# Linear attention followed by a mish feed-forward on one Trainium2 core: quarter-array key sums, later requests for v, reordered output products, a split first unit

## The chip, the cores and the metric

The kernel runs on one core of one Trainium2 chip. The metric is the device time in microseconds of one execution. A core has five engines with queues of their own: TensorE (PE, matmuls; its weight loads are listed as PEld), VectorE (DVE), ScalarE (ACT), GpSimd (POOL) and SyncE (SP, which here issues every DMA). Each engine works its queue in order and waits on semaphores for the others.

## The reference

q, k and v have 8 batches, 8 heads, 576 positions and 64 channels. Both q and k go through a feature map, and the attention is linear:

```
proj = x @ w_phi                                   # 64 -> 128 features
proj = proj - max(|proj|) over the features
phi  = concat(exp(proj), exp(-proj))               # 256 features
kv   = sum over s of phi(k)[s] * v[s];  z = sum over s of phi(k)[s]
out  = (phi(q) @ kv) / (phi(q) . z + 1e-6)
```

The result, as 4608 tokens of 512 channels, goes through a feed-forward: h = x @ w_in (512 to 2048), g = h * tanh(softplus(h)), out = g @ w_out (2048 to 512). Everything is float32.

## The kernel before

**Attention.** Two heads are handled together, so there are 32 head pairs of 576 keys. All keys of all pairs are laid end to end and cut into 144 tiles of 128 keys; a *unit* is four tiles (512 keys), and there are 36 units. A pair has 4.5 tiles, so every ninth tile holds 64 keys of one pair and 64 of the next: 16 such shared tiles. For unit n, `k_load` brings the keys (L270), `k_proj` multiplies them with w_phi into PSUM (L281, `project` L239, eight matmuls of 64 rows by 128 columns), `k_center` takes the maximum and subtracts it (L284, `center` L248, two VectorE operations over 1024 columns), `k_exp` makes both exponentials on ScalarE (L287), and `k_sum` adds phi(k) times v into the PSUM tile of the pair (L292). v has a column of ones behind its 64 channels, which gives z. Each matmul of `k_sum` is split by `halves` (L256) into two parts of 128 rows by 64 columns. A shared tile is run twice over its 128 rows, once for each pair; the host has put zeros into v where a key belongs to the other pair. `k_store` copies a finished pair to SBUF (L306). Queries go through the same steps (`q_load` to `q_store`), with transposes (`q_turn`, `q_out`) around the product with kv (`q_num`).

v is loaded a pair at a time by `v_load` (L274) into one of three buffers; keys and queries have three buffers each, the projection has two PSUM buffers (tag pp).

**Weights.** While attention runs, the feed-forward weights are converted into a high and a low part, 32 pieces in all (`weight_load` L135, `weight_ops` L140). Pieces with fp >= 2 are written to DRAM when both parts are there (`done` L223, store in L228) and come back later.

**Feed-forward.** A float32 product is made of three: high times high, high times low, low times high. `ff_in` (L435) makes h with seven block products, `first_product` and `winograd` combine them, `mish` applies the activation on ScalarE, `g_hi` (L509, ScalarE) and `g_lo` (L515, VectorE) split g into gh and gl, and `ff_out` (L561) multiplies with w_out. For each half (`which`) it fills two PSUM tiles with six products each, in the order gh wh, gh wl, gl wh, for the two blocks f of g.

**The order of the work** is written out by hand. Every step is an event with a nominal time, `at(time, step, ...)`; the events are sorted by it and issued in that order (L858 to L860), so the times set only the order on each engine's queue. The tables at L32 to L62 hold these times: L_AT for the four units ahead of the steady state (LEAD), K_AT and Q_AT for the key and query steps of a unit, which come STEP = 7.43 apart, CONV and WORD_AT for the weights, XS_AT and STEP1_AT for the feed-forward. The events of a unit are made in L685 to L715. All DMAs go through SP's one queue in this order, each with its own wait for a free buffer.

Of the kernel before, what the change touches and what calls it, by code (L numbers as in the profile page):

```python
# [12 lines left out]
ALU = mybir.AluOpType  # L13
# [24 lines left out]
Q_AT = (1.54, 3.27, 6.19, 6.49, 1.9, 3.04, 6.65, 10.0)  # L38
T_AT = (0.95, 2.0, 4.9, 5.3, 8.55, 10.92, 12.6, 13.1)
JOIN = 1.22  # L40
PRE = (11.72, 6.53)
CONV = (13.32, 14.93)
WORD_AT = 4.8
X0_AT = (37.79, 30.51)
RESUME = 38.35
FFSTEP = 10.6
HALF = 4
# [3 lines left out]
NXC = 9  # L51
FF2STEP = 8.01
TRAIL = 8.53
STEP1_AT = (0.75, 1.5, 1.53, 2.24, 5.7, 8.0, 6.24, 11.5, 12.7, 14.3, 18.4, 24.05)
XS_AT = (1.0, 10.69, 0.03, 4.92, 1.2)
# [13 lines left out]
def attention_then_mish(ctx, tc, qT, kT, va, w_phi, w_in, w_out, w_out2, out):  # L69
# [15 lines left out]
    nc.sync.dma_start(w_phi2, w_phi)  # L85
    ident = const.tile([P, P], F32, tag="ident", name="ident")
    make_identity(nc, ident)

# [51 lines left out]
    def weight_ops(kind, fp, k, quiet):  # L140
# [5 lines left out]
        def w():  # L146
            return piece[key][1][:, 0:4].rearrange("p b m -> p (b m)")
# [88 lines left out]
        return ops, rest_ops  # L236


    def project(raw, name):  # L239

        ps = ps_a.tile([P, 2, 4, F], F32, tag="pp", name=f"pp_{name}")
        for n in range(4):
            for j in range(2):
                rows = slice(j * D, (j + 1) * D)
                nc.tensor.matmul(ps[:, j, n], raw[rows, n * P:(n + 1) * P], w_phi2[rows], start=True, stop=True)  # L245
        return ps

    def center(ps, name):  # L248
        e = att.tile([P, 2, 2, 512], F32, tag="e", name=f"e_{name}", bufs=5)
        m = att.tile([P, 2, 4], F32, tag="m", name=f"m_{name}", bufs=4)  # L250
        nc.vector.tensor_reduce(m, ps, axis=AX.X, op=ALU.max, apply_absolute_value=True)  # L251
        nc.vector.tensor_tensor(e[:, :, 0, :].rearrange("p j (n f) -> p j n f", f=F), ps,  # L252
                                m.unsqueeze(3).broadcast_to([P, 2, 4, F]), op=ALU.subtract)
        return e

    def halves(ps, lhsT, rhs, start, stop):  # L256
# [8 lines left out]
    def pairs_of(t):  # L265

        for p in range(t * P // S, (t * P + P - 1) // S + 1):
            yield p, t - p * S // P

    def k_load(n):  # L270
        k_live[n] = att.tile([P, 512], F32, tag="kraw", name=f"kraw_{n}", bufs=3)
        nc.sync.dma_start(k_live[n], kT[n])

    def v_load(n):  # L274
        for t in range(4 * n, 4 * n + 4):
# [3 lines left out]
                    nc.sync.dma_start(v_live[p].rearrange("p t j w -> p (t j w)"), va[p])  # L279

    def k_proj(n):  # L281
        k_live[n] = project(k_live.pop(n), f"k_{n}")

    def k_center(n):  # L284
        k_live[n] = center(k_live.pop(n), f"k_{n}")

    def k_exp(n):  # L287
        e = k_live[n]
        nc.scalar.activation(e[:, :, 1, :], e[:, :, 0, :], AF.Exp)
        nc.scalar.activation(e[:, :, 0, :], e[:, :, 0, :], AF.Exp, scale=-1.0)  # L290

    def k_sum(n):  # L292
        es = k_live.pop(n)
        for i in range(4):
            for p, slot in pairs_of(4 * n + i):
                if slot == 0:
                    kv_ps[p] = ps_b.tile([P, 2, 2, VW], F32, tag="b", name=f"kvps_{p}")
                ps, vt = kv_ps[p], v_live[p]
                for j in range(2):
# [261 lines left out]
    def ff_out(n, which):  # L561
        s, sc, fp, first, last = steps[n]
        gh, gl = g_live[n]
        assert not any(("out", fp, k) in pieces_left for k in range(2))
        if first and which == 0:
            o_live[s] = [None] * 4
        assert stage[n, "u"] == 7
        for tt in (2 * which, 2 * which + 1):
            if first:
                o_live[s][tt] = ps_b.tile([P, DM], F32, tag="b", name=f"o_{s}_{tt}")  # L570
            ps = o_live[s][tt]
            cols = slice(tt % 2 * P, (tt % 2 + 1) * P)
            for f in range(2):
                wh, wl = wout[fp][:, f, 0], wout[fp][:, f, 1]
                h, l = gh[:, 2 * f + which, cols], gl[:, 2 * f + which, cols]
                for k, (g, w) in enumerate(((h, wh), (h, wl), (l, wh))):
                    nc.tensor.matmul(ps, g, w, start=(first and f == k == 0), stop=(last and f == 1 and k == 2))  # L577
        if which:
            del g_live[n]

# [167 lines left out]
    for i, pc in enumerate(pieces):  # L748
# [5 lines left out]
        at(clock - 12.0, weight_load, *pc)  # L754
        bits, sums = weight_ops(*pc, quiet)
        for delay, op in bits:
            at(clock - WORD_AT + delay, op)
# [141 lines left out]
```

## Time and profile before

| | us |
|---|---|
| median of 3 runs | 1041.77 (1040.81 to 1042.14) |
| profiled execution, its own time | 1043.07 |
| span of that execution, first to last instruction | 1041.3 |
| PE busy in the span | 1023.5 |
| DVE busy | 732.7 |
| ACT busy | 497.4 |
| POOL busy | 302.0 |

A line of the timeline gives the start in us, the duration, the engine, the line of the kernel, the operation, the tile written and the tiles read, the shape, and how often; in brackets stands the idle time of the engine ahead of it and what ended it. A line of the waits gives the engine and line that waited, what it waited for, the us in total, how many times, and the longest. "issue" is a wait for nothing that the profile shows. A line of the windows gives for a stretch from A to B its length and then the busy us of PE, PEld, DVE, ACT and POOL, each with a count, the granted TensorE clock (PEclk, 1.00 is full), the busy share of the DMA engines, and GB/s. A float32 matmul of the attention stage is two records in the trace, each with a weight load and a matmul.

### The profile page before, as it was taken

To read this page: it belongs to the slowest core of one execution; us is meant where nothing else is said; L and a number is where in the kernel's file an instruction comes from. 1 tells how busy PE (TensorE), PEld (TensorE's weight loads), DVE (VectorE), ACT (ScalarE), POOL (GpSimd) and SP (SyncE) were. 2 spreads that over 40 slices of the span, in tenths; PEclk is the share of its full clock that TensorE was granted. 3 is DMA by queue.
4 is the path that set the end of the run, shared out by engine and by line. 5 is a ranking of instruction groups with operands and counts; after the bars stand their busy time and mean duration, and the time that the engine had idled before them with its cause. 6 is when DMAs were issued, how large, how long until landed. Compare 5 with 4: busy or idle time off the path is not lost.

```text
span 1041.3 us, 27535 instructions
## 1 busy us (share of the span) xinstructions
PE 1023.5 (98%) x11848; PEld 970.8 (93%) x11848; DVE 732.7 (70%) x1158; ACT 497.4 (48%) x861; POOL 302.0 (29%) x263
## 2 busy tenths in 40 slices
PE   7999999999999999999999999999999999999998
PEld 7999899998989999999999999999999999999997
DVE  5888888887646987486674763367667677677665
ACT  4777777777754534344343533243333333333332
POOL 0545326533610555446553540000000000000000
PEclk9999999999999999999999999999999999999999
DMA  6545646666769576664855559982451542532621
GB/s 193 191 140 184 202 154 239 241 208 204 260 233 394 199 283 220 211 227 157 295 223 185 197 178 351 386 336 92 165 192 59 196 158 85 203 127 97 223 82 41
DMA packets 87081, 208.58 MB, mean 200 GB/s; under 512 B 6960, under 2 KB 34736, under 8 KB 84144
## 3 DMA queue, kind: packets, MB, share of 16 engines
q1 hardware_dynamic: 86960, 206.83, 56.4%
q8 instruction: 93, 1.52, 0.6%
q14 instruction: 28, 0.23, 0.1%
HBM read 122.91 MB, written 83.89 MB: 199 GB/s over the span
## 4 chain that ended last, share of the span: by engine, by line
PE 97%; DVE 1%; issue 1%; ACT 1%; DMA 0%; SPq 0%; DVEq 0%
PE h L449 34%; PE o L577 19%; PE o L598 17%; PE kvps L260 7%; PE num L260 7%; PE pp_k L245 4%; PE dt L328 3%; PE pp_q L245 3%; PE xt L371 2%; DMA kraw<-kT 0%; DVE m_k L251 0%; ACT L504 0%; DVE e_k L252 0%; DVE e_q L252 0%; DVE gl L518 0%
## 5 line engine op out<-in xcount | busy, mean ns | idle before, releaser
L449 PE MATMUL h<-xc,win 128*128 128x256 f32 x3024 | 381.5, 283 | 0.3 <-DVE u L477 0.3
L449 PEld LDWEIGHTS h<-xc,win 128*128 128x128 f32 x3024 | 375.3, 192 | 6.1 <-DVE u L477 0.5
L577 PE MATMUL o<-wout,gh 128*128 128x512 f32 x576 | 180.4, 395 | 0.2 <-ACT gh L512 0.2
L656 POOL TENSOR_TENSOR part<-part,du 128x512 f32<-128x512 f32 x18 | 23.4, 1298 | 387.9 <-DVE du L648 387.9
L577 PEld LDWEIGHTS o<-wout,gh 128*128 128x128 f32 x576 | 104.4, 190 | 18.7 <-ACT gh L512 0.4
L481 DVE TENSOR_TENSOR u<-h,u 128x512 f32<-128x512 f32 x72 | 49.6, 689 | 95.0 <-PE h L449 94.9
L577 PE MATMUL o<-wout,gl 128*128 128x512 f32 x288 | 112.8, 392 | 1.9 <-DVE gl L518 1.9
L598 PE MATMUL o<-wa,gh 128*128 128x256 f32 x576 | 104.4, 282 | 0.0
L456 ACT COPY p<-h 128x256 f32<-128x256 f32 x72 | 26.4, 367 | 134.0 <-PE h L449 134.0
L598 PEld LDWEIGHTS o<-wa,gh 128*128 128x128 f32 x576 | 88.6, 190 | 0.1
L260 PE MATMUL kvps<-v,e_k 128*64 128x65 f32 x2560 | 82.9, 224 | 4.0 <-issue 4.0
L260 PEld LDWEIGHTS kvps<-v,e_k 128*64 128x64 f32 x2560 | 79.3, 139 | 5.1 <-issue 4.4
L598 PE MATMUL o<-wa,gl 128*128 128x256 f32 x288 | 80.2, 283 | 0.0
L598 PE MATMUL o<-wb,held 128*128 128x256 f32 x648 | 79.3, 282 | 0.2 <-DVE du L648 0.2
L598 PEld LDWEIGHTS o<-wb,held 128*128 128x128 f32 x648 | 78.3, 188 | 0.4 <-DVE du L648 0.4
L334 ACT ACTIVATE e_q<-dt 128x512 f32<-128x512 f32 x144 | 74.3, 604 | 6.9 <-PE dt L328 6.8
L260 PE MATMUL num<-kv,e_q 128*64 128x65 f32 x2304 | 74.9, 223 | 0.0
L260 PEld LDWEIGHTS num<-kv,e_q 128*64 128x64 f32 x2304 | 70.1, 137 | 4.4 <-issue 0.3
L469 DVE TENSOR_TENSOR u<-h,p 128x256 f32<-128x256 f32 x72 | 30.2, 419 | 60.7 <-ACT p L456 60.7
L577 PEld LDWEIGHTS o<-wout,gl 128*128 128x128 f32 x288 | 54.4, 189 | 14.3 <-DVE gl L518 2.4
L251 DVE TENSOR_REDUCE m_k<-pp_k 128x8 f32<-128x1024 f32 x36 | 44.0, 1222 | 28.7 <-PE pp_k L245 28.7
L497 ACT ACTIVATE sb<-h 128x256 f32<-128x256 f32 x36 | 13.8, 384 | 105.0 <-PE h L449 71.1
(94 smaller groups left out, 1662.5 us busy)
## 6 DMA issues: line engine op xcount, KB each, us to landing
xc_spill<-xc SPq DMA_DIRECT2D x63, 512.0 KB, 4.6
xc<-xc_spill SPq DMA_DIRECT2D x63, 512.0 KB, 5.3
x<-x_spill SPq DMA_DIRECT2D x22, 512.0 KB, 7.0
o_part<-part SPq DMA_DIRECT2D x11, 1024.0 KB, 5.0
part<-o_part SPq DMA_DIRECT2D x11, 1024.0 KB, 5.9
in_spill<-wst_in SPq DMA_DIRECT2D x12, 896.0 KB, 4.4
win<-in_spill SPq DMA_DIRECT2D x12, 896.0 KB, 8.0
v<-va SPq DMA_DIRECT2D x32, 325.0 KB, 3.5
```

The costliest lines, as they stand in the source:

```text
L245: nc.tensor.matmul(ps[:, j, n], raw[rows, n * P:(n + 1) * P], w_phi2[rows], start=True, stop=True)
L251: nc.vector.tensor_reduce(m, ps, axis=AX.X, op=ALU.max, apply_absolute_value=True)
L260: nc.tensor.matmul(ps[rows], lhsT[:, rows], rhs[h], start=start, stop=stop, skip_group_check=True)
L328: nc.tensor.transpose(ps[:, i * P:(i + 1) * P], e[:, 0, i * P:(i + 1) * P], ident)
L334: nc.scalar.activation(e[:, s, :], ps, AF.Exp, scale=2.0 * s - 1.0)
L449: nc.tensor.matmul(ps, w, x, start=(i in (0, 2) and m == 0), stop=(m == 5), skip_group_check=True)
L456: nc.scalar.copy(p1, h_live[n][0][:, 0])
L469: nc.vector.tensor_tensor(u2, hx[:, 1], u_live[n][0], op=ALU.add)
L481: nc.vector.tensor_tensor(u[:, 0:3:2] if second(n) else u[:, 1:3], hy, u2.unsqueeze(1).broadcast_to([P, 2, CH]), op=ALU.add)
L577: nc.tensor.matmul(ps, g, w, start=(first and f == k == 0), stop=(last and f == 1 and k == 2))
L598: nc.tensor.matmul(ps, g, w, start=(start and k == 0), stop=(stop and k == 2), skip_group_check=True)
L656: nc.gpsimd.tensor_tensor(cross, cross, d_live[s, tau][0].unsqueeze(1).broadcast_to([P, 2, CH]), op=ALU.add)
```

## The change

Four edits, with retimed events.

1. `k_sum` takes the tiles of a unit with one pair first and the shared tile last. In a shared tile rows 0 to 63 go to the first pair and rows 64 to 127 to the second, as matmuls of 64 rows by 64 columns, in turn.
2. LOAD_AT sets the times of the loads: k_load at 11.1 ahead of the unit's time (before: 1.5 x 7.43 = 11.1), v_load at 1.0 ahead (before: 0.8 x 7.43 = 5.94), q_load at 9.59 (before: 8.92), the weights' words at 12.68 (before: 12.0). The store of a converted weight piece is two DMAs: the high part when it is written, the low part when that is.
3. `ff_out` makes all eight products with gh, and then the four with gl.
4. The first two tiles' columns of the first key unit come with w_phi in one DMA (`head`), the other two by k_load(0). The first unit is projected into two PSUM buffers, and centered and exponentiated in two halves.

The tables L_AT, K_AT, Q_AT, T_AT, CONV, X0_AT, XS_AT, STEP1_AT, LEAD_STEP and JOIN get other values. On PE's queue this moves one step: the projections of unit 4 and of the first query come ahead of k_sum(2). On ACT's queue mish(n, 1) comes ahead of first_product(n + 1) in most feed-forward steps, and on VectorE's some x_sum, x_block and drain steps change places with their neighbours.

```diff
-LEAD_STEP = 3.28
-L_AT = (0.0, 0.95, 3.4, 7.0, 9.38)
+LEAD_STEP = 2.8
+L_AT = (0.0, 2.62, 3.19, 7.71, 9.38)
-K_AT = (0.94, 1.9, 3.04, 3.85, 4.24)
+LOAD_AT = (-11.1, -1.0, -9.59, -12.68)
+K_AT = (0.94, 1.9, 3.62, 3.69, 4.24)
-JOIN = 1.22
+JOIN = 0.99
-X0_AT = (37.79, 30.51)
+X0_AT = (38.06, 28.03)
...
-    w_phi2 = const.tile([P, F], F32, tag="w_phi", name="w_phi2")
-    nc.sync.dma_start(w_phi2, w_phi)
+    head = const.tile([P, 3, F], F32, tag="head", name="head")
+    nc.sync.dma_start(head, w_phi)
+    w_phi2 = head[:, 0]
...
             nc.scalar.copy(dst[:, 0], piece[key][1][:, 1:8] if blocks else w())
+            spill(0)
...
+            spill(1, dst)
+
+        def spill(h, dst=None):
+            dst = piece[key][3] if dst is None else dst
             if fp >= 2:
...
-                nc.sync.dma_start(where, dst.bitcast(F32))
+                nc.sync.dma_start(where[:, h], dst[:, h].bitcast(F32))
...
+        for a, b, ps in parts:
+            nc.vector.tensor_reduce(m[:, :, a:b], ps[:, :, a:b], axis=AX.X, op=ALU.max, apply_absolute_value=True)
+            nc.vector.tensor_tensor(to[:, :, a:b], ps[:, :, a:b],
+                                    m[:, :, a:b].unsqueeze(3).broadcast_to([P, 2, b - a, F]), op=ALU.subtract)
...
+    def cuts_of(n):
+        return (0, 4) if n else (0, 2, 4)
...
     def k_sum(n):
         es = k_live.pop(n)
-        for i in range(4):
-            for p, slot in pairs_of(4 * n + i):
-                if slot == 0:
+        tiles = [list(pairs_of(t)) for t in range(4 * n, 4 * n + 4)]
+        for i in sorted(range(4), key=lambda i: len(tiles[i])):
+            fresh = []
+            for p, slot in tiles[i]:
+                if p not in kv_ps:
                     kv_ps[p] = ps_b.tile([P, 2, 2, VW], F32, tag="b", name=f"kvps_{p}")
-                ps, vt = kv_ps[p], v_live[p]
-                for j in range(2):
-                    for s in range(2):
-                        halves(ps[:, j, s], es[:, j, s, i * P:(i + 1) * P], (vt[:, slot, j, :],) * 2,
-                               start=(slot == j == s == 0), stop=(slot == 4))
+                    fresh.append(p)
+            shared = len(tiles[i]) == 2
+            for j in range(2):
+                for s in range(2):
+                    for r, (p, slot) in enumerate(tiles[i]):
+                        rows = slice(r * D, (r + 1) * D) if shared else slice(0, P)
+                        halves(kv_ps[p][:, j, s], es[rows, j, s, i * P:(i + 1) * P], (v_live[p][rows, slot, j, :],) * 2,
+                               start=(p in fresh and j == s == 0), stop=(slot == 4))
...
+        for g, ks in ((gh, (0, 1)), (gl, (0,))):
+            for tt in (2 * which, 2 * which + 1):
+                cols = slice(tt % 2 * P, (tt % 2 + 1) * P)
+                for f in range(2):
+                    for k in ks:
+                        nc.tensor.matmul(o_live[s][tt], g[:, 2 * f + which, cols], wout[fp][:, f, k],
...
-        at(t - 1.5 * STEP, k_load, u)
-        at(t - 0.8 * STEP, v_load, u)
+        at(t + (LOAD_AT[0] if u >= LEAD else -11.1), k_load, u)
+        at(t + (LOAD_AT[1] if u >= LEAD else -5.9), v_load, u)
...
-        at(t - 1.2 * STEP - early, q_load, u)
+        at(t + LOAD_AT[2] - early, q_load, u)
```

More of the change, by code (lines that the diff above doesn't have):

```diff
@@ L32 @@
 LEAD = 4
[L33 to L34 removed]
+LEAD_STEP = 2.8
+L_AT = (0.0, 2.62, 3.19, 7.71, 9.38)
 STEP = 7.43
 TAIL_STEP = 5.73
[L37 to L40 removed]
+LOAD_AT = (-11.1, -1.0, -9.59, -12.68)
+K_AT = (0.94, 1.9, 3.62, 3.69, 4.24)
+Q_AT = (1.54, 3.19, 6.19, 6.49, 1.9, 3.04, 6.65, 9.16)
+T_AT = (0.95, 2.19, 4.9, 5.3, 8.55, 10.92, 12.6, 13.1)
+JOIN = 0.99
 PRE = (11.72, 6.53)
[L42 to L44 removed]
+CONV = (13.48, 14.91)
+WORD_AT = 4.79
+X0_AT = (38.06, 28.03)
 RESUME = 38.35
@@ L53 @@
 TRAIL = 8.53
-STEP1_AT = (0.75, 1.5, 1.53, 2.24, 5.7, 8.0, 6.24, 11.5, 12.7, 14.3, 18.4, 24.05)
-XS_AT = (1.0, 10.69, 0.03, 4.92, 1.2)
+STEP1_AT = (0.75, 1.5, 1.53, 2.24, 5.7, 7.36, 6.24, 11.21, 12.7, 14.3, 18.4, 24.05)
+XS_AT = (1.0, 10.83, 0.28, 5.83, 1.2)
 XBACK_AT = (-3.05, 1.0, 1.7, 2.4, 3.1, 5.2, 5.66)
@@ L236, in weight_ops, with project, center @@
         return ops, rest_ops
-    def project(raw, name):
-        ps = ps_a.tile([P, 2, 4, F], F32, tag="pp", name=f"pp_{name}")
-        for n in range(4):
-            for j in range(2):
[L244 to L248, printed above, removed]
+    def project(raw, name, cuts=(0, 4)):
+        parts = []
+        for a, b in zip(cuts, cuts[1:]):
+            ps = ps_a.tile([P, 2, 4, F], F32, tag="pp", name=f"pp_{name}_{a}")
+            parts.append((a, b, ps))
+            for n in range(a, b):
+                for j in range(2):
+                    rows = slice(j * D, (j + 1) * D)
+                    src = head[rows, 1 + n] if b < 4 else raw[rows, n * P:(n + 1) * P]
+                    nc.tensor.matmul(ps[:, j, n], src, w_phi2[rows], start=True, stop=True)
+        return parts
+    def center(parts, name):
         e = att.tile([P, 2, 2, 512], F32, tag="e", name=f"e_{name}", bufs=5)
         m = att.tile([P, 2, 4], F32, tag="m", name=f"m_{name}", bufs=4)
-        nc.vector.tensor_reduce(m, ps, axis=AX.X, op=ALU.max, apply_absolute_value=True)
-        nc.vector.tensor_tensor(e[:, :, 0, :].rearrange("p j (n f) -> p j n f", f=F), ps,
-                                m.unsqueeze(3).broadcast_to([P, 2, 4, F]), op=ALU.subtract)
+        to = e[:, :, 0, :].rearrange("p j (n f) -> p j n f", f=F)
+        for a, b, ps in parts:
+            nc.vector.tensor_reduce(m[:, :, a:b], ps[:, :, a:b], axis=AX.X, op=ALU.max, apply_absolute_value=True)
+            nc.vector.tensor_tensor(to[:, :, a:b], ps[:, :, a:b],
+                                    m[:, :, a:b].unsqueeze(3).broadcast_to([P, 2, b - a, F]), op=ALU.subtract)
         return e
@@ L288, in k_exp @@
         e = k_live[n]
-        nc.scalar.activation(e[:, :, 1, :], e[:, :, 0, :], AF.Exp)
-        nc.scalar.activation(e[:, :, 0, :], e[:, :, 0, :], AF.Exp, scale=-1.0)
+        for a, b in zip(cuts_of(n), cuts_of(n)[1:]):
+            cols = slice(a * P, b * P)
+            nc.scalar.activation(e[:, :, 1, cols], e[:, :, 0, cols], AF.Exp)
+            nc.scalar.activation(e[:, :, 0, cols], e[:, :, 0, cols], AF.Exp, scale=-1.0)
     def k_sum(n):
         es = k_live.pop(n)
-        for i in range(4):
-            for p, slot in pairs_of(4 * n + i):
-                if slot == 0:
-                    kv_ps[p] = ps_b.tile([P, 2, 2, VW], F32, tag="b", name=f"kvps_{p}")
-                ps, vt = kv_ps[p], v_live[p]
-                for j in range(2):
-                    for s in range(2):
-                        halves(ps[:, j, s], es[:, j, s, i * P:(i + 1) * P], (vt[:, slot, j, :],) * 2,
-                               start=(slot == j == s == 0), stop=(slot == 4))
+        tiles = [list(pairs_of(t)) for t in range(4 * n, 4 * n + 4)]
[3 more added lines that the diff above has]
+                if p not in kv_ps:
+                    kv_ps[p] = ps_b.tile([P, 2, 2, VW], F32, tag="b", name=f"kvps_{p}")
+                    fresh.append(p)
+            shared = len(tiles[i]) == 2
+            for j in range(2):
+                for s in range(2):
[3 more added lines that the diff above has]
+                               start=(p in fresh and j == s == 0), stop=(slot == 4))
+            for p, slot in tiles[i]:
                 if slot == 4:
@@ L570, in ff_out @@
                 o_live[s][tt] = ps_b.tile([P, DM], F32, tag="b", name=f"o_{s}_{tt}")
[L571 to L577, printed above, removed]
+        for g, ks in ((gh, (0, 1)), (gl, (0,))):
[4 more added lines that the diff above has]
+                        nc.tensor.matmul(o_live[s][tt], g[:, 2 * f + which, cols], wout[fp][:, f, k],
+                                         start=(first and g is gh and f == k == 0), stop=(last and g is gl and f == 1),
+                                         skip_group_check=True)
         if which:
@@ L753, in attention_then_mish @@
             clock = CONV[0] + CONV[1] * i
-        at(clock - 12.0, weight_load, *pc)
+        at(clock + (LOAD_AT[3] if 0 < i < 4 * HALF else -12.0), weight_load, *pc)
         bits, sums = weight_ops(*pc, quiet)
@@ L871 @@
     kT = k.reshape(B, NHP, 2, S, D).transpose(2, 4, 0, 1, 3).reshape(P, -1, 512).transpose(1, 0, 2)
-    w2 = np.concatenate([w_phi, w_phi])
+    w2 = np.concatenate([np.concatenate([w_phi, w_phi]), kT[0, :, :2 * P]], axis=1).reshape(P, 3, F)
     va = np.zeros((B, NHP, 5 * P, 2, VW), np.float32)
```

5 lines of the change are left out of this document (3 added, 2 removed).

## The prediction

> **What bounds the kernel now.** I read the page's busy shares first, then the chain of work that ended last, then what TensorE (PE) waited for.
>
> ```profile
> span 1041.3 us, 27535 instructions
> ...
> PE 97%; DVE 1%; issue 1%; ACT 1%; DMA 0%; SPq 0%; DVEq 0%
> PE h L449 34%; PE o L577 19%; PE o L598 17%; PE kvps L260 7%; PE num L260 7%; PE pp_k L245 4%; PE dt L328 3%; PE pp_q L245 3%; PE xt L371 2%; DMA kraw<-kT 0%; DVE m_k L251 0%; ACT L504 0%; DVE e_k L252 0%; DVE e_q L252 0%; DVE gl L518 0%
> ...
> L577 PE MATMUL o<-wout,gh 128*128 128x512 f32 x576 | 180.4, 395 | 0.2 <-ACT gh L512 0.2
> ...
> L577 PE MATMUL o<-wout,gl 128*128 128x512 f32 x288 | 112.8, 392 | 1.9 <-DVE gl L518 1.9
> ...
> L260 PE MATMUL kvps<-v,e_k 128*64 128x65 f32 x2560 | 82.9, 224 | 4.0 <-issue 4.0
> ```
>
> PE is the chain for 97% of the span, so a change pays only where it shortens PE's own work, fills PE's few waits, or keeps its clock up. The list of PE's waits names nearly all of them:
>
> ```profile
> PE pp_k L245 <- DMA kraw<-kT: 4.0, 1, 4.0
> PE kvps L260 <- issue: 4.0, 3, 1.6
> PE o L577 <- DVE gl L518: 1.9, 1, 1.9
> PE pp_q L245 <- PE pp_k L245: 1.0, 2, 0.6
> ```
>
> Stretches of one clock period (3.41 us) show one more loss: PEclk 0.50 from 303.56 on, right after a stretch in which PE was busy 1.26 of 3.41 us. After a stretch with 2.20 us busy the clock stayed full.
>
> ```profile
> core 0: us, PE busy (x) PEld busy (x) DVE busy (x) ACT busy (x) POOL busy (x), PEclk, DMA share, GB/s
> ...
> 248.94:252.36 3.42, 2.20 (x74) 2.06 (x71) 2.98 (x5) 2.35 (x4) 2.64 (x3) 1.00 0.62 237
> ...
> 300.15:303.56 3.41, 1.26 (x7) 0.62 (x6) 2.84 (x4) 3.38 (x6) 0.00 (x0) 1.00 0.66 217
> 303.56:306.97 3.41, 3.41 (x9) 2.65 (x10) 3.11 (x5) 1.83 (x4) 0.00 (x0) 0.50 1.05 343
> ```
>
> **Part 1, gh products ahead of gl's (ff_out).** Nothing is added or removed: eight gh products, then four gl products, in place of gh, gh, gl four times.
>
> ```profile
> 300.75 0.73 PE L577 MATMUL o<-wout,gh 128*128 128x512 f32 x2 [0.23 <-ACT gh L512]
> ...
> 302.13 1.22 DVE L518 TENSOR_TENSOR gl<-u,gh 128x1024 fp32r<-128x1024 f32 x1
> ...
> 303.40 0.68 PE L577 MATMUL o<-wout,gl 128*128 128x512 f32 x1 [1.92 <-DVE gl L518]
> ```
>
> One product costs 19% of 1041.3 us over 576 + 288, 0.229 us. Today two of them run before the wait; now eight do, so 6 x 0.229 = 1.37 us of the 1.92 is filled and 0.55 stays, because gl still ends at 302.13 + 1.22 = 303.35. What is late next is that same gl. The stretch from 300.15 would then hold 1.26 + 1.37 = 2.63 us of PE work, more than the 2.20 that kept the clock, so the half clock should go: half of 3.41, 1.71 us. Sum -3.1. Ends: -1.4 (the clock still drops) and -3.6 (gl comes early enough for the whole wait). In the later steps there is no wait of this kind to win: the row above has 1.9 us in all 288.
>
> **Part 2, v requested later, weight stores in two parts.** The three waits "issue" of kvps lie inside runs of matmuls that have all their data. Around the first:
>
> ```profile
> 97.07 0.33 SPq L279 DMA_DIRECT2D v<-va  x1
> ...
> 98.88 0.50 SPq L316 DMA_DIRECT2D qraw<-qT  x1
> ...
> 106.26 1.28 PE L260 MATMUL kvps<-v,e_k 128*64 128x65 f32 x36 [1.54 <-issue]
> ```
>
> ```profile
> 98.50:103.00 4.50, 4.50 (x97) 4.21 (x97) 3.67 (x4) 2.45 (x6) 0.30 (x1) 1.00 0.93 323
> 103.00:106.26 3.26, 1.72 (x61) 1.63 (x55) 2.73 (x8) 3.03 (x6) 1.33 (x1) 1.00 0.13 42
> ```
>
> ```profile
> q8 instruction: 1, 0.02, 1.8%
> ```
>
> The last line is the DMA view of 103.0 to 106.2; from 98.5 to 103.0, at a DMA share of 0.93, there is no such packet. So PE ran out of instructions while their fetch stood behind five data transfers (v, words_out, x_spill, kraw, qraw) that SP issued in one burst, 97.07 to 98.88. The burst comes from the first of them:
>
> ```profile
> SPq L279 <- PE kvps L260: 111.4, 25, 8.3
> ```
>
> v waits on SP for the buffer that an earlier k_sum frees, 25 times and 111.4 us in all, and everything behind it waits along. The change moves v_load 4.94 us back (from 0.8 x 7.43 = 5.94 ahead of the unit's time to 1.0). By the order's own times the k_sum that frees its buffer starts 3.7 us ahead of that time, so v will mostly find its buffer free, and the issues spread out; of the weight stores the first half goes when ACT's copy is there, which halves the largest single transfers. I take two of the three waits as gone: 4.0 x 2/3 = -2.7. Ends: 0 and -4.0. Moving v costs nothing while it lands in time: it is now asked for 1.0 + 7.43 + 3.69 = 12.1 us of the order's time ahead of its k_sum and lands within 6.9 us at worst; without that cover each late v stops PE.
>
> ```profile
> DMA to landing us min/median/max: 2.8/3.5/6.9
> ```
>
> The 24 extra store issues on SP (about 0.4 us each, as the rows above) queue ahead of transfers that have microseconds of slack.
>
> **Part 3, shared key tiles as four parts (k_sum).** 16 of the 144 key tiles belong to two head pairs. Each was run twice over 128 rows with zeros in v; now rows 0 to 63 go to one pair, 64 to 127 to the other. The count stays: of the 2560 records, 160 (tile, pair) sums make 16 each, so 16 x 2 x 16 = 512 belong to shared tiles.
>
> ```profile
> 95.87 1.96 PEld L260 LDWEIGHTS kvps<-v,e_k 128*64 128x64 f32 x64
> ...
> 97.89 0.86 PEld L328 LDWEIGHTS dt<-ident,e_q 128*128 128x128 f32 x8
> ...
> 98.72 0.47 PEld L371 LDWEIGHTS xt<-ident,x 128*128 128x128 f32 x4
> ...
> 99.36 0.97 PEld L245 LDWEIGHTS pp_k<-w_phi,kraw 64*128 64x128 f32 x16 [0.17 <-issue]
> ...
> 100.24 0.98 PEld L245 LDWEIGHTS pp_q<-w_phi,qraw 64*128 64x128 f32 x16
> ...
> 101.34 1.95 PEld L260 LDWEIGHTS num<-kv,e_q 128*64 128x64 f32 x64
> ```
>
> A kvps record takes 1.96/64 = 30.6 ns for 65 columns, a pp_k record 0.97/16 = 60.6 ns for 128, a dt record, which fills the array, 0.86/8 = 107 ns for 128. So half-array parts run two at a time, and time goes with columns. If four quarter parts run four at a time, a record takes 15.3 ns: 512 x 15.3 = -7.8. If they start no faster than now: 0. No row shows a quarter part; no row shows starts closer than 30 ns on average either, so I stay short of the halving: 21 ns, 512 x 9.6 = -4.9. Against it stands one more change of array shape per shared tile (it is sorted to the end of its unit). Where the shape changes, weight loading stops for 0.06 (97.83 to 97.89), 0.17 (99.19 to 99.36) and 0.12 us (101.22 to 101.34): 16 x 0.12 = +1.9 (1.0 to 2.7). Sum -3.0; ends -6.8 and +2.7.
>
> **Part 4, the first unit in halves, packed with w_phi, and the new lead order.**
>
> ```profile
> 0.72 0.39 SPq L85 DMA_DIRECT2D w_phi<-w_phi  x1
> 1.16 0.89 SPq L272 DMA_DIRECT2D kraw<-kT  x2
> ...
> 4.05 3.79 PE L245 MATMUL pp_k<-w_phi,kraw 64*128 64x128 f32 x32 [4.05 <-DMA kraw<-kT]
> ...
> 8.75 2.08 PE L245 MATMUL pp_k<-w_phi,kraw 64*128 64x128 f32 x16 [0.92 <-PE pp_k L245]
> ...
> 25.75 1.16 PE L245 MATMUL pp_q<-w_phi,qraw 64*128 64x128 f32 x16 [0.63 <-PE pp_k L245]
> ...
> 31.41 1.16 PE L245 MATMUL pp_q<-w_phi,qraw 64*128 64x128 f32 x16 [0.36 <-PE pp_k L245]
> ```
>
> ```profile
> w_phi<-w_phi SPq DMA_DIRECT2D x1, 64.0 KB, 1.9
> ```
>
> ```profile
> L481 DVE TENSOR_TENSOR u<-h,u 128x512 f32<-128x512 f32 x72 | 49.6, 689 | 95.0 <-PE h L449 94.9
> ```
>
> The first product now needs 192 KB in one transfer. 64 KB had landed by 0.72 + 1.9 = 2.6, 256 KB more by 4.0; in proportion 192 KB lands at 3.3: -0.7. VectorE then starts on half a unit. Against that, unit 0 takes both PSUM buffers of the projection, so unit 1's projection waits for the first half's centering (two operations of half size, 0.69 us each by the row above, against 8 x 0.118 = 0.94 us of PE's second half): +0.45, in place of the 0.92 above. Unit 4 and the first query are projected before k_sum(2), not after, and q_load(0) no longer queues behind v; VectorE gets its work earlier, which should end the waits of 0.63 and 0.36. Sum -0.7 + 0.45 - 0.92 - 0.99 = -2.2. Ends: 0 (the 192 KB come no earlier than all of it did) and -3.9: early records take 3.79/32 = 118 ns, twice the later 60.6, so a clock that rises one period earlier would give 1.7 more.
>
> **What is moved at no cost.** In the feed-forward stage ACT runs mish(n,1) ahead of the next first_product, and x_sum, x_block and drain change places on VectorE. PE is busy 373.03 of 373.03 us there; a step's ACT and VectorE work is done two steps ahead of its output products, which covers 0.85 us of mish.
>
> ```profile
> 306.97:680.00 373.03, 373.03 (x2344) 338.24 (x2343) 241.29 (x371) 155.56 (x256) 152.02 (x128) 1.00 0.70 253
> ```
>
> Without that cover it would cost 0.85 us in each of 34 steps.
>
> **Sum.** -3.1 - 2.7 - 3.0 - 2.2 = -11.0. The profiled execution took 1043.07 us (its span of 1041.3 and 1.8 around it), 1.3 above the median; against its own time the sum gives 1032.1. I take the same difference off the median of 1041.77: **1030.8 us**.
>
> **The rivals.** (A) *The four parts gain nothing.* For it: no row has records closer than 30 ns on average; against it: two parts do overlap. Price 4.9: 1035.7. The Trainium skill, "TensorE: Matmul & The Clock Gate", section "Wait — 56ns, not 53.3ns?", says that starts of small matmuls never come closer than about 25 ns; by that figure the parts would win 2.9 by estimate and part 3 would be -1.0. No record here is short enough to test it. (B) *The fetch waits stay or move*: the DMA share is over half in the attention stage whatever the order, against it the bursts behind v. 1030.8 + 2.7 = 1033.5. (C) *The clock still drops at 303*: 1032.5; against it the 2.20 us stretch. (D) *Slower.* Two parts with the same columns write the same PSUM partitions, if in two banks; if they cannot overlap there and each part runs alone, a record takes 61 ns: 512 x 30.6 = +15.7 in place of -4.9, 1051.4. It makes the kernel slower from 43 ns a record on (the other parts' 8.0 less 1.9 leaves 6.1, 512 x 12 ns). Against it: column parts of one bank overlap today. (E) *It does not do what it says*: v still waits, gl's wait only moves: 1041.8.
>
> **Chances.** Forecast 0.55, A 0.20, B 0.12, C 0.07, D 0.03, E 0.03. The forecast's own range, from a few of the ends at once, is 1027 to 1034. Down to 1026 takes in the early clock or the full halving of part 3, up to 1037 takes in A with B in part. Under 0.2% (2.1 us) cannot be told from no change. Faster is all but D, E and some of A with B: 0.93; same 0.03; slower 0.04.
>
> **What would show it.** Right: no half clock near 300, PE's wait for gl near 0.5 us; SP's wait of L279 for kvps down from 111 us and at most one "issue" wait over 0.5 us; 64x64 records of kvps at 20 ns or so; first product near 3.3. Wrong: kvps quarter records at 30 ns or more, a PE wait for v, or a new wait of pp_q in the first 30 us.

## The result, and the profile after

| | us |
|---|---|
| median before, 6 runs of one session | 1040.88 (1039.86 to 1042.14) |
| median of the changed kernel, 6 runs | 1033.74 (1031.03 to 1037.98) |
| ratio | 0.993, 95% interval 0.9914 to 0.9946 |
| profiled execution of the changed kernel, its own time | 1037.98 |
| span of that execution | 1036.2 |

The change makes the kernel 7.1 us faster, to 1033.7. Forecast were 11.0 us and 1030.8; the kernel before came out 0.9 us lower here than the 1041.77 that the forecast started from. The profiled execution is the longest of the six, and its rows must be read with that in mind. The page of the changed kernel, its span, busy line and chain:

```profile
span 1036.2 us, 27630 instructions
...
PE 1019.5 (98%) x11848; PEld 965.2 (93%) x11848; DVE 731.2 (71%) x1160; ACT 496.9 (48%) x863; POOL 305.9 (30%) x263
...
PE 94%; DMA 2%; ACT 1%; DVE 1%; issue 1%; SPq 0%; DVEq 0%
PE h L475 34%; PE o L602 18%; PE o L625 17%; PE num L273 7%; PE kvps L273 6%; PE pp_k L256 4%; PE dt L354 3%; PE pp_q L256 3%; PE xt L397 1%; DMA x<-x_spill 1%; DMA qraw<-qT 1%; DMA head<-w_phi 0%; ACT e_k L310 0%; ACT e_k L309 0%; ACT e_q L360 0%
```

PE is busy 4.0 us less (1023.5 before). That is not the price of the shared tiles, since PE's busy time also holds its stretches at half clock, and these differ between the two executions (below). Two new names stand in the chain, the load of x and the load of queries, 1% of the span each, where before no transfer but the first had a place. The list of PE's waits in the changed kernel:

```profile
PE kvps L273 <- issue: 4.7, 4, 2.4
PE pp_k L256 <- DMA head<-w_phi: 3.3, 1, 3.3
PE h L475 <- DVE u L495: 1.5, 1, 1.5
PE pp_k L256 <- DVE e_k L265: 0.7, 1, 0.7
PE o L602 <- ACT gh L538: 0.7, 1, 0.7
PE o L602 <- DVE gl L544: 0.6, 1, 0.6
```

The wait for gl fell from 1.92 to 0.55, the first product starts at 3.27 instead of 4.05, and the waits of pp_q are gone. But the fetch waits ("issue") are not: 4.7 us here, against 4.0. And there is a new wait, h for u, 1.5 us. (The kernel before has one wait of h for u, 0.3 us at 298.82, ahead of the first output product; behind that product, where this one stands, it has none.) SP's queue in the same kernel:

```profile
SPq L405 <- ACT xs L404: 85.7, 24, 6.9
...
SPq L235 <- ACT wst_in L209: 65.5, 11, 10.9
...
SPq L297 <- PE kvps L273: 39.1, 15, 11.0
```

v's wait (L297, L279 before) went from 111.4 to 39.1 us. The stores of weights and of transposed tokens (L235, L405) now wait longer instead.

Why this execution is long shows in the windows of one clock period (A to B, length, PE busy, clock, DMA share, GB/s), behind the longest fetch wait, 2.36 us from 25.2 on:

```profile
core 0: us, PE busy (x), PEclk, DMA share, GB/s
...
23.91:27.33 3.42, 1.33 (x45) 1.00 0.98 333
27.33:30.74 3.41, 3.14 (x19) 0.50 0.82 285
30.74:34.16 3.42, 3.42 (x38) 0.50 0.05 17
```

The wait left 1.33 us of work in its period, and two periods at half clock followed. So the half clock near 303 is gone, as forecast, and another one came at 27. The same kernel in a second session (the experiment "a_again") was profiled with a span of 1030.5 and these waits:

```profile
PE kvps L273 <- issue: 1.8, 2, 1.0
PE h L475 <- DVE u L495: 1.4, 1, 1.4
...
PE o L602 <- ACT gh L538: 0.7, 1, 0.7
PE o L602 <- DVE gl L544: 0.5, 1, 0.5
```

Fetch waits are 2.9 us shorter and there is no half clock from the first rise to the last microseconds. 2.9 and half of two periods (3.4) make 6.3; the two spans lie 5.7 apart. The clock's first rise goes the other way: PE's records of kvps shrink from 315 to 222 ns at 10.3 us in the first profile and at 11.0 in the second, which is 0.4 us of work. In these three things the two executions differ; the waits of h, e_k, gh and gl repeat within 0.1 us.

Where the gain arises: the start of four events on PE and the span, read from the timeline of each profile.

| | before | changed, profiled first | changed, a_again |
|---|---|---|---|
| first product | 4.05 | 3.27 | 3.31 |
| first output product (o, gh) | 300.75 | 296.50 | 290.91 |
| step 84: h after the first output products | 310.14 | 302.93 | 297.34 |
| step 168: two half steps later | 328.44 | 323.25 | 317.59 |
| span | 1041.3 | 1036.2 | 1030.5 |

(Step n is the matmul of h that has n others ahead of it.) From the first output product to step 84 the kernel takes 9.39 us before and 6.43 after: 2.96 gained, against the 3.1 of part 1. Over the next stretch, to step 168, it takes 18.30 before and 20.32 or 20.25 after: 2.0 lost again. From step 168 to the end nothing differs by more than 0.15 us.

### The profile page after: what moved, and what is told of

It is laid out like the page before. It is cut to its first block, busy times and chain, and to the rows that moved or that the text cites. A ratio compares the mean times of both kernels' runs of the same rounds, so it can differ in the third digit from the quotient of the medians.

```text
span 1036.2 us, 27630 instructions
## 1 busy us (share of the span) xinstructions
PE 1019.5 (98%) x11848; PEld 965.2 (93%) x11848; DVE 731.2 (71%) x1160; ACT 496.9 (48%) x863; POOL 305.9 (30%) x263
## 4 chain that ended last, share of the span: by engine, by line
PE 94%; DMA 2%; ACT 1%; DVE 1%; issue 1%; SPq 0%; DVEq 0%
PE h L475 34%; PE o L602 18%; PE o L625 17%; PE num L273 7%; PE kvps L273 6%; PE pp_k L256 4%; PE dt L354 3%; PE pp_q L256 3%; PE xt L397 1%; DMA x<-x_spill 1%; DMA qraw<-qT 1%; DMA head<-w_phi 0%; ACT e_k L310 0%; ACT e_k L309 0%; ACT e_q L360 0%
## 5 line engine op out<-in xcount | busy, mean ns | idle before, releaser
L602 PE MATMUL o<-wout,gh 128*128 128x512 f32 x576 | 144.3, 392 | 0.7 <-ACT gh L538 0.7
L273 PE MATMUL kvps<-v,e_k 128*64 128x65 f32 (+1 forms) x2560 | 77.5, 223 | 4.7 <-issue 4.7
L273 PEld LDWEIGHTS kvps<-v,e_k 128*64 128x64 f32 (+1 forms) x2560 | 72.6, 137 | 7.0 <-issue 5.5
L602 PE MATMUL o<-wout,gl 128*128 128x512 f32 x288 | 77.1, 389 | 0.6 <-DVE gl L544 0.6
L264 DVE TENSOR_REDUCE m_k<-pp_k 128x8 f32<-128x1024 f32 (+1 forms) x37 | 44.1, 1193 | 24.5 <-PE pp_k L256 24.5
```

Source lines behind the costliest of these rows:

```text
L264: nc.vector.tensor_reduce(m[:, :, a:b], ps[:, :, a:b], axis=AX.X, op=ALU.max, apply_absolute_value=True)
L273: nc.tensor.matmul(ps[rows], lhsT[:, rows], rhs[h], start=start, stop=stop, skip_group_check=True)
L602: nc.tensor.matmul(o_live[s][tt], g[:, 2 * f + which, cols], wout[fp][:, f, k], start=(first and g is gh and f == k == 0), stop=(last and ...
```

## The experiments

Kernels named b_ are the kernel before with one part of the change; those named a_ are the changed kernel with one part undone or shifted. Three sessions; each kernel is compared with the kernel before of its own session (medians 1041.69, 1042.72 and 1042.51). The retimed tables other than LOAD_AT, LEAD_STEP and L_AT stand in none of the kernels b_ and in all of the kernels a_, so that no run shows what they are worth.

### The product order alone (b_gh)

```diff
-            for f in range(2):
...
-                for k, (g, w) in enumerate(((h, wh), (h, wl), (l, wh))):
+        for g, ks in ((gh, (0, 1)), (gl, (0,))):
+            for tt in (2 * which, 2 * which + 1):
```

> The kernel before with the new order of products in ff_out alone (eight gh, then four gl). My theory: PE's one wait for gl shrinks from 1.9 us to about 0.55, the half clock from 303.6 to 307.0 us is gone, and the kernel is 3.1 us faster. Rival 1: the clock still drops, 1.4 us faster. Rival 2: PE arrives earlier at the feed-forward stage than its data do, so part of the 3.1 us comes back as a new PE wait there (the changed kernel has one of 1.5 us, for a VectorE step behind the load of x), about 1.6 us faster.

Measured: 1041.23, ratio 0.9994 (0.998 to 1.0009), -0.5 us. The half clock near 303 is absent, the wait for gl is 0.5, and the stretch to step 84 is 2.94 us shorter: the mechanism is as forecast. But 1.65 of it is lost before step 168, at a wait of h for u (L469) of 1.1 us that the kernel before does not have, so more than half of the gain is given back in the next stretch.

### The four parts alone (b_quarter)

```diff
+        for i in sorted(range(4), key=lambda i: len(tiles[i])):
...
-                        halves(ps[:, j, s], es[:, j, s, i * P:(i + 1) * P], (vt[:, slot, j, :],) * 2,
...
+                    for r, (p, slot) in enumerate(tiles[i]):
+                        rows = slice(r * D, (r + 1) * D) if shared else slice(0, P)
+                        halves(kv_ps[p][:, j, s], es[rows, j, s, i * P:(i + 1) * P], (v_live[p][rows, slot, j, :],) * 2,
```

> The kernel before with the new k_sum alone: the shared tile last, in parts of 64 rows by 64 columns. My theory: the 512 records of shared tiles fall from 30.6 to about 20 ns, less one more change of array shape per tile, so about 3 us faster. Rival 1: the parts start no closer than 30 ns, and the kernel is about 2 us slower. Rival 2: PE's gain in the attention stage is taken back by waits for instruction fetches, which the DMA traffic sets, and the time does not change by more than 1 us though the records are shorter.

Measured: 1042.15 (1039.15 to 1047.5), ratio 1.001 (0.9994 to 1.0025): no gain, though the parts themselves are fast (below). PE's waits in this kernel show transfers that were in time before:

```profile
PE pp_k L245 <- DMA kraw<-kT: 5.0, 2, 4.0
PE kvps L260 <- issue: 2.2, 3, 1.0
...
PE pp_q L245 <- DMA qraw<-qT: 1.6, 1, 1.6
```

Beside the first load there is a second wait for keys (5.0 - 4.0 = 1.0) and one for a query (1.6). The wait for keys ends at 8.8 us, before any k_sum has run, and stands where the kernel before waited 0.92 for pp_k, so it is no loss of this part. The wait for the query, at 20.88, comes of the new order of the tiles. The first query is requested right behind the v that takes over the buffer of pair 0, and that buffer is free when the shared tile of k_sum(1) has been read. Start of k_sum(1) and of that v, before and in b_quarter:

```profile
15.15 4.42 PE L260 MATMUL kvps<-v,e_k 128*64 128x65 f32 x144
15.87 0.33 SPq L279 DMA_DIRECT2D v<-va  x1
```

```profile
13.93 4.26 PE L260 MATMUL kvps<-v,e_k 128*64 128x65 f32 x144
16.20 0.33 SPq L279 DMA_DIRECT2D v<-va  x1
```

With the shared tile first v follows 0.72 us into k_sum(1), with the shared tile last 2.27 us. b_gh has the old order and runs as early (k_sum(1) at 14.10, v at 14.82), and has no such wait. The prediction did not count this cost of sorting the shared tile to the end. That profile is of a quick execution (1040.16); what the longest ones, up to 1047.5, waited for was not traced.

### The load times and two-part stores alone (b_loads)

```diff
+LOAD_AT = (-11.1, -1.0, -9.59, -12.68)
...
-                nc.sync.dma_start(where, dst.bitcast(F32))
+                nc.sync.dma_start(where[:, h], dst[:, h].bitcast(F32))
```

> The kernel before with the new load times and the two-part weight stores alone. My theory as predicted: SP's wait for v falls from 111 us, one or two of the three PE waits 'issue' over 0.5 us vanish, 2.7 us faster. Rival: SP now waits for ACT's high part instead of for v (in the changed kernel 104 us at the store line), the transfers behind it still go out in bursts, the fetch waits only change place, and the time is within 1 us of before.

Measured: 1037.97, ratio 0.9968 (0.9957 to 0.9979), -3.7 us. The only part that gains by itself. In its profile kvps waits for instructions 0.3 us in place of 4.0, and pp_k 1.2. It also holds two half-clock periods, whose windows show how little work it takes:

```profile
7.61:11.02 3.41, 1.54 (x22) 1.00 0.94 277
11.02:14.44 3.42, 3.16 (x58) 0.50 0.14 50
...
297.74:301.15 3.41, 1.51 (x7) 1.00 1.03 332
301.15:304.57 3.42, 3.42 (x10) 0.50 0.97 286
```

### The start alone (b_head)

```diff
-LEAD_STEP = 3.28
-L_AT = (0.0, 0.95, 3.4, 7.0, 9.38)
+LEAD_STEP = 2.8
+L_AT = (0.0, 2.62, 3.19, 7.71, 9.38)
...
+    head = const.tile([P, 3, F], F32, tag="head", name="head")
```

> The kernel before with the packed first load, the first unit in halves and the new order of the first four units alone. My theory: first product near 3.3 us instead of 4.05, no PE waits of 0.63 and 0.36 us ahead of pp_q, 2.2 us faster. Rival: PE runs ahead of the instruction fetches in the first 30 us (the changed kernel waited 2.4 us at 25 us and then had half clock for 6.8 us), so the gain varies from run to run and its median is under 1 us.

Measured: 1041.73, ratio 0.9996 (0.9982 to 1.001): no difference that can be measured, between -1.9 and +1.0 us. The first product comes at 3.16, but its profile has 4.6 us of fetch waits (kvps 3.0, pp_q 1.6) in place of 4.0, and 0.5 for later keys.

The four parts alone come to -0.5 + 0.5 - 3.7 + 0.0 = -3.7 us; together they give 7.1 to 9.9. Either the parts depend on each other, then, or the rest of the change, the other retimed tables, has a share. The next sessions undo the parts one by one from the changed kernel.

### The changed kernel again (a_again)

The same code, so that the next three have it beside them.

> The changed kernel once more, beside its own variants on the same chip. Expected: about 7 us faster than before, a second profile with the half clock near 300 us gone and with the PE wait of about 1.5 us behind the load of x near 316 us; if the 2.4 us fetch wait at 25 us was one execution's, it is absent here and the profiled time lies near 1032 us.

Measured: 1032.87 (1031.79 to 1035.09), ratio 0.9909 (0.9888 to 0.993), -9.9 us. With the six runs of the result its twelve runs have a median of 1033.2; the six of the result had two of 1037.7 and 1038.0, the second of them the profiled one with the half clock at 27.

### Without the four parts (a_noquarter)

```diff
-                    for r, (p, slot) in enumerate(tiles[i]):
-                        rows = slice(r * D, (r + 1) * D) if shared else slice(0, P)
...
+                        halves(ps[:, j, s], es[:, j, s, i * P:(i + 1) * P], (vt[:, slot, j, :],) * 2,
```

> The changed kernel with the old k_sum (both passes over 128 rows). My theory now: with the load times of the change in place PE is no longer held by the fetches, so the shorter records count, and without them the time rises by about 3 us (16 tiles, 32 records each at 10 ns, less the change of array shape). Rival: as on the kernel before, where they alone moved nothing, the fetches take the gain back, and the time rises by under 1 us.

Measured: 1036.9 (1035.31 to 1038.4), ratio 0.9943 (0.9924 to 0.9962). All six runs lie above all six of a_again; the parts are worth 4.0 us here. The price of a shared tile stands in the weight loads of a unit with one, first before, then in a_again (the timeline puts the two shapes of such a unit into one row):

```profile
49.89 2.42 PEld L260 LDWEIGHTS kvps<-v,e_k 128*64 128x64 f32 x80
```

```profile
46.11 1.95 PEld L273 LDWEIGHTS num<-kv,e_q 128*64 128x64 f32 x64
47.97 2.11 PEld L273 LDWEIGHTS kvps<-v,e_k 128*64 128x64 f32 x80
```

48 half-array records at 1.95/64 = 30.5 ns are 1.46 us, so the 32 quarter records and the change of shape take 0.65, where 32 half-array records took 0.96: 0.31 us a tile, 16 x 0.31 = 5.0 us. Record by record, quarter parts start 15.4 ns apart on average (median over the sixteen tiles): four within 20 ns, one for each quarter of the array, and the next four 58 ns after the first of these. The first of all starts 152 ns behind the last half-array one. Half-array records start in pairs, 58 ns from pair to pair. The groups of the changed kernel by shape show all 512:

```profile
L273 PE MATMUL kvps<-v,e_k 128*64 128x65 f32 x2048 | 66.9, 222 | 2.6 <-issue 2.6
...
L273 PE MATMUL kvps<-v,e_k 64*64 64x65 f32 x512 | 11.7, 224 | 2.2 <-issue 2.2
```

Their sum of 78.6 compares with 81.3 us for 2560 half-array records in a_noquarter; busy time counts the overlapping tail of a run as well, so the weight loads give the better price. Of the 5.0 us, 4.0 arrive in the time. In its profile a_noquarter has no fetch wait over 0.15 us, a_again has 1.8 us of them; so the faster records may be paying some of their gain back there, but with one profile of each that is not shown.

### With the old start (a_nohead)

```diff
-LEAD_STEP = 2.8
-L_AT = (0.0, 2.62, 3.19, 7.71, 9.38)
+LEAD_STEP = 3.28
+L_AT = (0.0, 0.95, 3.4, 7.0, 9.38)
...
-    head = const.tile([P, 3, F], F32, tag="head", name="head")
```

> The changed kernel with the old start (w_phi alone, the first unit whole, the old order of the first four units). My theory: the time rises by 0 to 2 us, since the earlier start is partly given back within the first 100 us. Rival: the earlier start makes PE outrun its fetches and drops the clock in some executions, so without it the median is the same or lower and the runs lie closer together than 1031 to 1038.

Measured: 1035.35 (1034.99 to 1036.29), ratio 0.993 (0.9913 to 0.9948): the start is worth 2.5 us on the changed kernel, more than the 0 to 2 expected. The rival was right in one thing, that the runs lie closer together: within 1.3 us, those of a_again within 3.3. PE's waits are the old ones again:

```profile
PE pp_k L251 <- DMA kraw<-kT: 4.1, 1, 4.1
...
PE pp_q L251 <- PE pp_k L251: 1.3, 2, 0.9
PE kvps L266 <- issue: 1.2, 2, 0.6
PE pp_k L251 <- PE pp_k L251: 0.9, 1, 0.9
```

4.1 + 1.3 + 0.9 = 6.3, against 3.3 for the first load and 0.7 for e_k in the changed kernel: 2.3 us. The clock's first rise comes at 12.4 us here and at 11.0 in a_again; whether that belongs to the start or to the execution is open (below, part 4).

### One x_sum later (a_xsum)

The wait of h for u was the loss after step 84, and it hangs on a load of x. From the profile of the changed kernel:

```profile
303.99 2.42 SPq L421 DMA_DIRECT2D x<-x_spill  x2
...
314.97 0.69 DVE L434 TENSOR_TENSOR xs<-x 128x512 f32<-128x512 f32 x1 [3.38 <-DMA x<-x_spill]
...
317.51 0.42 DVE L495 TENSOR_TENSOR u<-h,p 128x256 f32<-128x256 f32 x1
317.98 2.20 PE L475 MATMUL h<-xc,win 128*128 128x256 f32 x14 [1.49 <-DVE u L495]
```

The load is issued at 304.0 to 306.4 and VectorE stands 3.38 us for it at 314.97; its four subtractions then come ahead of u, and h's matmuls need u. The experiment puts the subtractions of that one segment behind the u of this step:

```diff
-            at(t + XS_AT[1] + XS_AT[2] * i, x_sum, s, i)
+            at(t + XS_AT[1] + XS_AT[2] * i + (2.2 if s == 2 else 0.0), x_sum, s, i)
```

> The changed kernel with the four x_sum steps of the third segment 2.2 of the order's time later, so that VectorE does winograd of the fourth step ahead of them. My theory: the PE wait of 1.5 us near 316 us (h for VectorE's u, which stands behind x_sum and with it behind the load of x) is gone, and the kernel is 1.5 us faster than the changed one. Rival: the late load of x, not the place of x_sum, holds the stage; the wait only moves to gl or to the next x blocks, and the time stays.

Measured: 1032.7, ratio 0.9908 (0.9888 to 0.9927), the same as a_again. The wait is gone where it was (from step 126 to 168 it takes 10.53 us, as the kernel before does), and a new one of 0.8 us stands at the next segment's x_sum; by step 420, 1.27 us are lost against the kernel before. The wait had only moved.

### Both x_sums later (a_best)

```diff
+            at(t + XS_AT[1] + XS_AT[2] * i + (2.2 if s in (2, 3) else 0.0), x_sum, s, i)
+        t = t_of(n - 1) if n >= AHEAD + 2 else begin - (X0_AT[1], 3.6)[s]
```

> The changed kernel with x_sum of the third and fourth segments 2.2 later in the order and the x blocks of the second segment 0.3 later, so that ScalarE writes gh(0) ahead of the first block and VectorE writes gl(0) ahead of the second. My theory: PE's waits for gh (0.7 us) and gl (0.5 us) at the first output product and both waits for VectorE's u behind x_sum are gone: 2 to 2.5 us faster than the changed kernel, if the load of x keeps up. Rival: the load of x is the bound there; what PE gains at the first output product comes back as a wait for x later, and the time stays within 0.5 us.

Measured: 1032.42, ratio 0.9911 (0.9896 to 0.9925): not to be told from the changed kernel. The wait moved again, now to the blocks made from those sums:

```profile
PE h L475 <- DVE xc L444: 1.3, 1, 1.3
```

Three orders, three places, 1.3 to 2.0 us lost each time. The DMA share in a_again is 0.90 to 1.06 in every clock period from 290.9 to 308.0, which speaks for the transfers as what sets the pace there and not the order on VectorE; no run with fewer transfers tested that.

### With the old product order (a_oldgg)

> The changed kernel with the old order of products in ff_out. My theory: the wait for gl is 1.9 us again, the half clock near 300 us is back (3.0 us lost until the third step), and the wait behind the load of x near 316 us goes (2.0 us won back): about 1 us slower than the changed kernel. Rival: the new order is worth its full 3.1 us here.

The edit of b_gh, reversed:

```diff
-        for g, ks in ((gh, (0, 1)), (gl, (0,))):
-            for tt in (2 * which, 2 * which + 1):
...
+                for k, (g, w) in enumerate(((h, wh), (h, wl), (l, wh))):
```

Measured: 1033.27, ratio 0.9914 (0.9899 to 0.9928), beside a_again's 0.9909: on the changed kernel the product order is worth 0.5 us by the ratios, inside both intervals. The wait for gl is back:

```profile
291.94 0.73 PE L603 MATMUL o<-wout,gh 128*128 128x512 f32 x2 [0.73 <-ACT gh L538]
294.59 0.50 PE L603 MATMUL o<-wout,gl 128*128 128x512 f32 x1 [1.92 <-DVE gl L544]
```

```profile
292.78:296.19 3.41, 1.60 (x7) 1.00 1.00 331
296.19:299.60 3.41, 3.41 (x17) 1.00 0.98 301
```

But this time the clock stays: the same 1.92 us wait fell across two periods so that the poorer one held 1.60 us of work. From the first output product to step 84 this kernel takes 7.77 us, 1.34 more than a_again; to step 168 from there 18.85, 1.40 less, since its h waits 0.4 us for u (in the row of its weight loads) instead of 1.4. The two cancel.

### With v's old time (a_vearly)

```diff
-LOAD_AT = (-11.1, -1.0, -9.59, -12.68)
+LOAD_AT = (-11.1, -5.94, -9.59, -12.68)
```

> The changed kernel with v requested 5.94 ahead of the unit's time, as before, and all else kept. My theory: SP's wait for v is back near 100 us, the five-transfer bursts with it, and the three fetch waits; 3 to 4 us slower than the changed kernel. Rival: the later v is not what counts; the two-part stores are, and the time stays within 1 us.

Measured: 1036.59 (1034.3 to 1041.29), ratio 0.9952 (0.9932 to 0.9972): 3.7 us more than a_again and than a_onestore of its own session (4.5 than a_again by the ratios). The waits of PE and, last, of SP for v's buffer:

```profile
PE kvps L273 <- issue: 2.4, 4, 0.8
...
PE pp_k L256 <- DMA kraw<-kT: 1.2, 1, 1.2
...
PE pp_q L256 <- DMA qraw<-qT: 0.8, 1, 0.8
```

```profile
SPq L297 <- PE kvps L273: 103.5, 26, 9.7
```

SP's wait for v is at 103.5 again, and the keys and queries queued behind v are late (2.0 us): the load of the keys that PE waits for at 22.5 goes out at 18.30, in a_again at 16.12. The 0.6 us more of fetch waits show nothing, since these range from 0 to 4.7 us in the profiles with v late. All waits of PE over 0.1 us but the first add up to 8.5 us here and to 5.8 in a_again; 1.5 of the 4.2 between the two spans is not in such waits and was not found.

### With single weight stores (a_onestore)

```diff
-            spill(0)
...
-            spill(1, dst)
+            spill(slice(0, 2), dst)
```

> The changed kernel with each weight store in one transfer again. My theory: SP waits less for ScalarE (104 us at the store line in the changed kernel), the single stores are larger again, and the time is within 1 us of the changed kernel. Rival: the halves are what spreads the transfers; 2 us or more slower, with fetch waits of over 0.5 us back.

Measured: 1032.9, ratio 0.9915 (0.9899 to 0.9932): the two-part stores neither gain nor cost anything that can be measured. So v's time alone accounts for part 2; the shifts of 0.67 us for the queries and 0.68 for the words were not taken back by themselves.

## Why the prediction was right or wrong

**Total.** The sign was right, and 1033.74 lies in the range of 1026 to 1037, 2.9 above the forecast. The terms were sized less well than their sum, and that the sum came near is in part luck: part 1 is short by 2.6 where parts 2, 3 and 4 are over by 1.0, 1.0 and 0.3, and the sum took for granted that the parts add up. Undone one at a time on the changed kernel they are worth:

| | forecast | alone, on the kernel before | undone, on the changed kernel |
|---|---|---|---|
| part 1, product order | -3.1 | -0.5 | -0.5 (not told from 0) |
| part 2, v later, stores in two | -2.7 | -3.7 | -3.7 (v), 0.0 (stores) |
| part 3, shared tiles as four parts | -3.0 | +0.5 | -4.0 |
| part 4, start | -2.2 | 0.0 | -2.5 |
| sum | -11.0 | -3.7 | -10.7 |

**Part 1: mechanism right, its gain lost in the next stretch.** What the part was to do, it did: 2.96 us in place of 3.1 to step 84, the wait for gl at 0.5 as forecast, no half clock. Two steps failed. The one is "moved at no cost": I took PE's 373.03 busy of 373.03 us in the later feed-forward as proof of cover. But a PE that never waits does not show by how much its data are ahead of it. In the trace of the kernel before this stood in three rows that I had not looked at:

```profile
319.02 0.69 DVE L408 TENSOR_TENSOR xs<-x 128x512 f32<-128x512 f32 x1 [0.22 <-DMA x<-x_spill]
321.56 0.42 DVE L469 TENSOR_TENSOR u<-h,p 128x256 f32<-128x256 f32 x1
323.54 2.32 PE L449 MATMUL h<-xc,win 128*128 128x256 f32 x18
```

VectorE already waited for the load of x, and the u behind it ended at 321.98, 1.56 us ahead of the h that needs it. The load did not come earlier with PE: it is requested 7.5 us behind the first output product before and after. So of the 2.96 us that PE gains 1.56 can be kept, and 1.40 come back as a wait of h for u; measured are 1.43 and 1.49. (From step 84 to 168 the loss is 2.0, since the later matmuls of that h wait for the next parts of u.) The other step is the 1.71 for the clock: a_oldgg keeps its clock with the same wait, so this term depends on where the wait falls in the clock's periods.

**Part 2: right in size, the mechanism only in part.** v's time alone gives the 3.7, between the -2.7 taken and the end of -4.0. The forecast took all of it from fetch waits. These do get fewer: 3.3 us on average in the five profiles with v early (2.2 to 4.6), 1.9 in the nine with v late (0 to 4.7), with ranges that overlap. The other effect, which the sum left out, is that keys and queries come in time: 2.0 us of waits for them in a_vearly, none behind the first 7 us in any profile with v late. "At most one issue wait over 0.5 us" was wrong: the first profile has three, the second two. They come and go between executions, so a count of them in one profile is no price. The two-part stores, which I had counted among the causes, are worth nothing.

**Part 3: under-sized.** I stopped at 21 ns a record since no row showed starts closer than 30 ns on average; they come 15.4 ns apart on average, the halving that the row of 64-row parts had suggested. The extra change of shape costs the 0.12 us assumed (152 ns start to start, against 29 within a run). 512 x 13.6 ns less 16 x 0.12 us makes 5.0; 4.0 is measured. Rivals A (the parts gain nothing) and D (parts on the same PSUM partitions wait for each other) fall by the same rows. A stood beside a rule of the Trainium skill, "TensorE: Matmul & The Clock Gate", section "Wait — 56ns, not 53.3ns?", that starts of small matmuls come no closer than about 25 ns. The records here do not agree: four parts that go to different quarters of the array start within 20 ns. The kernel before could already have tested it, against what the prediction says: its half-array records start in pairs 8 to 10 ns apart, which a mean of 30 ns hides.

**Part 4: right in size, term by term.** First product 4.05 to 3.27 or 3.31 (-0.7 forecast); the wait of unit 1 for the first half 0.71 (0.45); the waits of 0.92, 0.63 and 0.36 gone. 2.3 us by the rows, 2.5 measured. The end that I had put on an earlier rise of the clock belongs to the execution as well as to the start: with the old start matmul records reach their short length at 13.4 us (before) and 12.4 (a_nohead), but in b_gh and b_quarter already by 9.2; with the new one between 8.9 (b_head) and 11.0 (a_again). Half of such a difference is work lost or won, by estimate up to 2 us, without any change of the kernel.

**What I had not asked: whether the terms add up.** On the kernel before, parts 3 and 4 alone gain nothing; undone from the changed kernel they are worth 4.0 and 2.5. Some of what stands between is in the rows: in b_quarter the query that waits 1.6 us behind a v whose buffer is freed later, in b_head 4.6 us of fetch waits, so that Rival B's condition, that fetch waits move rather than go, held there. It held in part for the changed kernel: 4.7 us in one execution, 1.8 in another. But the changed kernel differs from these two by v's time, by the other parts and by the other retimed tables, and no run puts one of the parts together with v's time alone. So what the parts needed in order to pay stays open. As for the 2.9 us by which the time missed the forecast, the two runs near 1038 of the first six raise that median, and only one of them was profiled; in the second session the change is worth 9.9 us, 1.1 short of the 11.0, with part 1 short by 2.6.

## What to carry to other kernels

Before you price a wait as filled, follow the engine on to its next dependence on a transfer that does not move with it, and read how long its data lie ready there: here 1.56 us, so that of 2.96 us gained 1.4 came back. When one edit looks worthless by itself on a kernel that is bound by one engine, undo it from the whole change too before you drop it: here the same edits were worth 0 and 4.0, or 0 and 2.5. Ask of a new order not only what it speeds up but which buffer it frees later. And a tile whose two halves belong to different sums is better run in quarter-array parts than twice over its full height with zeros, as long as the change of shape (0.12 us) is paid once for a run of 32 of them (5.0 us here by the weight loads, 4.0 by the time).

## What the hardware showed that was not expected

A float32 record of 65 columns keeps its part of the array for about 58 ns, whether the part is 64 or 128 rows high: half-array records start in pairs every 58 ns, quarter-array records in fours every 58 ns (29 and 15.4 ns a record on average). So the four quarters run side by side, also the two that write the same PSUM partitions, in two PSUM tiles.

The granted clock followed the work of the last 3.41 us period. From full it fell to half behind periods with 1.26, 1.33, 1.48, 1.49, 1.51 and 1.54 us of PE work (before, the changed kernel, b_head, b_quarter, and two in b_loads) and stayed behind one with 1.60 (a_oldgg) and all with more. It came back after one period in all of these but the changed kernel, where it stayed at half for a second one though PE was busy 3.14 of 3.41 us in the first; why is not shown. A wait of 1.92 us therefore cost 1.7 us more or nothing, by where the period's edge cut it. So did the fetch wait near 25 us: 2.36 us left 1.33 in one period of the changed kernel, 2.38 us in a_oldgg left 2.39 and 2.06 of work in two, and the clock stayed.

The fetch waits of PE come at places that the code fixes. Of the 43 waits "issue" over 0.15 us in the fourteen profiles, 41 stand behind 475 matmul records of PE, counted from its first, or a multiple of 126 records later, within two. Behind record 475 the changed kernel waited 2.36 us in one execution and 0.99 in the other, its variants 0.56 (a_xsum), 0.15 (a_best), 2.38 (a_oldgg) and 0.56 (a_onestore). What changes between executions is which of these places costs time. It is more likely where data transfers fill the DMA engines (share 0.98 in the period of the 2.36 us wait), but most places pass without a wait: from record 475 on, 15 of 84 waited where the DMA share of the 4 us ahead was 0.9 or more, and none of 25 where it was under 0.1.
